# Random-feature attention: key and query products by halves of their stationary columns, values copied into rows of 65

## The chip, the cores and the metric

The kernel runs on one core of one Trainium2 chip. The metric is the device time of one execution in microseconds (us). Five engines with instruction streams of their own work together: TensorE (PE in the rows; its weight loads are PEld), VectorE (DVE), ScalarE (ACT), GpSimd (POOL) and SyncE (SP), whose queue issues the transfers. Each engine takes its own instructions in program order and waits on semaphores.

## The reference

Three parts follow each other: attention with positive random features, then a layer with `h - tanh(h)`, then four experts whose outputs are added with weights. Only the attention is touched:

```python
q_s, k_s = (q * scale, k * scale)
def phi(x):
    proj = np.einsum('bhsd,md->bhsm', x, omega)
    sq = np.sum(x * x, axis=-1, keepdims=True) / 2.0
    h = proj - sq
    h = h - np.max(h, axis=-1, keepdims=True)
    return np.exp(h) / np.sqrt(m)
q_p, k_p = (phi(q_s), phi(k_s))
kv = np.einsum('bhsm,bhsd->bhmd', k_p, v)
z = np.sum(k_p, axis=2)
num = np.einsum('bhsm,bhmd->bhsd', q_p, kv)
den = np.einsum('bhsm,bhm->bhs', q_p, z)[..., None] + 1e-06
return (num / den).astype(np.float32)
```

There are 2 batches, 8 heads, 576 rows, a head size of 64 and 128 features; everything is float32.

## The kernel before

Heads go in four pairs (p = 0 to 3). A batch's 576 rows are four tiles of 128 tokens and a rest of 64; the two batches' rests share one tile, so there are nine token tiles. The key stage runs first, pair by pair. `features` transposes the keys (tile `psT`), splits them into a high and a low part (`th` on ACT, `tl` on DVE), projects them (`psP`), takes the maximum (`nm` on DVE) and the exponent (`kf` on ACT). `k_products` then multiplies the features with the values: for each batch and head five float32 matmuls accumulate into `psV`, with 128 feature columns of `kf` stationary and 128 moving columns, 64 of them values and 64 of them ones, so that the sum z comes out beside kv. A DVE copy takes 96 of those 128 columns into `kvz[p]`.

The values lie in two tiles, `vs_105` for even pairs and `vs_106` for odd ones. Four transfers for a pair, a large one (line 199) and a small one for the rest rows (line 237) per batch, write straight into them, and the ones stand at the end of the same tile; `v_ones` makes the moving operand as a pattern of two blocks of 64. Pair p + 2 may be loaded once the matmuls of pair p have read the tile.

The query stage works on twelve units (a head pair and a third of the tiles). `turned` transposes query features (`psQ`, copied to `qt` on ACT); `attended` multiplies `qt` with `kvz` into `psN`: 128 stationary token columns and 96 moving columns for a tile of one batch (line 348). For the tile that holds both batches' rests it makes two matmuls of 64 stationary columns and 65 moving ones (line 352), one into the upper and one into the lower half of the partitions. DVE divides (`rd`, `xs`), and `back` turns the result over (`psX`).

Beside the key stage the first weights of the next layer are loaded into `raw` and decoded (ACT line 111, DVE lines 122, 126 and 127, split on ACT and POOL), and beside the query stage the first hidden products of that layer (`pse`, line 437) already run on PE. In these stages the order on each engine is decided by a scheduler from the program's dependences; in the layers behind them it is written by hand on PE, DVE and ACT.

Of the kernel before, what the change touches and what calls it, by code (L numbers as in the profile page):

```python
# [8 lines left out]
F32 = mybir.dt.float32  # L9
# [17 lines left out]
def tile_favor_attention__then__two_moe(  # L27
# [18 lines left out]
    nc = tc.nc  # L46
    B, H, S, D = q.shape
# [4 lines left out]
    P = 128  # L52
    NP = H // 2
    NT = N // P
    TB = S // P
# [14 lines left out]
    def split(hi, lo, src, eng_lo=None):  # L70
        nc.scalar.activation(hi, src, AF.Copy)
        (eng_lo or nc.vector).tensor_tensor(out=lo, in0=src, in1=hi.bitcast(F32), op=ALU.subtract)  # L72
# [110 lines left out]
    ac = actx.enter_context(tc.tile_pool(name="ac", bufs=1))  # L183
# [6 lines left out]
    kp = kctx.enter_context(tc.tile_pool(name="kp", bufs=2, side="right"))  # L190
    TD = TB * D
    VC = D + 1
    ZC = D + D // 2
    FULL = slice(0, TB * P)
    REST = slice(TB * P, S)

    def load_full(x, b, p, to):

        nc.sync.dma_start(out=to, in_=x[b, 2 * p:2 * p + 2, FULL, :].rearrange("h (r t) d -> r h (t d)", t=TB))
# [21 lines left out]
    kr = rests(k, "kr", kp)  # L221


    VR, VO = B * 2 * TD, B * 2 * (TD + D)
    vs = [kp.tile([P, VO + 3 * D], F32, tag=f"vs{i}", name=f"vs{i}", bufs=1) for i in range(2)]
    for i in range(2):
        nc.gpsimd.memset(vs[i][:, VR:], 0.0)
        nc.gpsimd.memset(vs[i][:, VO:VO + D], 1.0)
        for b in range(B):
            nc.gpsimd.memset(vs[i][b * D:(b + 1) * D, VO + (1 + b) * D:VO + (2 + b) * D], 1.0)  # L230

    def load_v(p):
        t = vs[p % 2]
        for b in range(B):
            load_full(v, b, p, t[:, b * 2 * TD:(b + 1) * 2 * TD].rearrange("p (h x) -> p h x", h=2))
            r = t[b * D:(b + 1) * D, VR + b * 2 * D:VR + (b + 1) * 2 * D].rearrange("p (h d) -> p h d", h=2)
            nc.sync.dma_start(out=r, in_=v[b, 2 * p:2 * p + 2, REST, :].rearrange("h r d -> r h d"))

    def v_ones(p, b, h, i):

        v0 = (b * 2 + h) * TD + i * D if i < TB else VR + (b * 2 + h) * D
        one = VO if i < TB else VO + (1 + b) * D
        x = vs[p % 2][:, v0:v0 + D]
        return bass.AP(x.tensor, x.offset, [x.ap[0], (one - v0, 2), x.ap[1]])

    load_v(0)
    kn.append(load_k(1))
    load_v(1)

    pso = ps_t.tile([P, 512], F32, tag="t", name="pso")  # L250
# [6 lines left out]
    for j in range(2):  # L257
        r, c = slice(j * D, (j + 1) * D), slice(j * P, (j + 1) * P)
        split(ob[0][r, c], ob[1][r, c], oms[r, :])
    qn = ac.tile([P, B, H, TD], F32, name="qn")  # L260
    kvz = [ac.tile([P, B, 2, ZC], F32, name=f"kvz{p}") for p in range(NP)]


    groups = [(0, 2), (2, 2), (TB, 1), (TB + 1, 2), (TB + 3, 2)]
# [43 lines left out]
    def k_products(p, kf):  # L308

        ps = ps_n.tile([P, B, 2, P], F32, tag="n", name="psV")  # L310

        def product(b, h):
            for i in range(TB + 1):
                nc.tensor.matmul(
                    ps[:, b, h, :], kf[:, TB if i == TB else b * (TB + 1) + i, h, :], v_ones(p, b, h, i),
                    start=i == 0, stop=i == TB,
                )
            if (b, h) == (B - 1, 1):
                nc.vector.tensor_copy(kvz[p], ps[:, :, :, :ZC])
                if p + 2 < NP:  # L320
                    load_v(p + 2)

        return [lambda b=b, h=h: product(b, h) for b in range(B) for h in range(2)]

    def q_products(p, gs, qf):

        nt = sum(n for _, n in gs)
        base = gs[0][0]
        xs = a3.tile([P, TB, 2, D], F32, tag="xs", name="xs")
        qt = {}  # L330

        def turned(g):
            t0, c = gs[g]
            ps = ps_t.tile([P, 2, 2, P], F32, tag="t", name="psQ")
            for j in range(c):
                for h in range(2):
                    nc.tensor.transpose(ps[:, j, h, :], qf[:, t0 - base + j, h, :], ident)
            qt[g] = a3.tile([P, 2, 2, P], F32, tag="qt", name="qt", bufs=4)
            nc.scalar.activation(qt[g][:, :c], ps[:, :c], AF.Copy)

        def attended(g):
            t0, c = gs[g]
            ps = ps_n.tile([P, 2, 2, P], F32, tag="n", name="psN")
            for j in range(c):
                t = t0 + j
                for h in range(2):
                    if t != TB:
                        nc.tensor.matmul(ps[:, j, h, :ZC], qt[g][:, j, h, :], kvz[p][:, t // (TB + 1), h, :], start=True, stop=True)  # L348
                        continue
                    for b in range(B):  # L350
                        r = slice(b * D, (b + 1) * D)
                        nc.tensor.matmul(ps[r, j, h, :VC], qt[g][:, j, h, r], kvz[p][:, b, h, :VC], start=True, stop=True)
            rd = a3.tile([P, 2, 2, 1], F32, tag="rd", name="rd")
            nc.vector.tensor_scalar(out=rd[:, :c], in0=ps[:, :c, :, D:VC], scalar1=1e-6 * M, scalar2=None, op0=ALU.add)
            nc.vector.reciprocal(rd[:, :c], rd[:, :c])
            nc.vector.tensor_tensor(
                out=xs[:, t0 - base:t0 - base + c], in0=ps[:, :c, :, :D], in1=rd[:, :c].to_broadcast([P, c, 2, D]), op=ALU.mult
            )

        def back():  # L360
            ps = ps_t.tile([P, 512], F32, tag="t", name="psX")
            for i in range(nt):
                nc.tensor.transpose(ps[:, i * P:(i + 1) * P], xs[:, i].rearrange("p h d -> p (h d)"), ident)
            c = slice(base * P, (base + nt) * P)
            split(xT[p][0][:, c], xT[p][1][:, c], ps[:, :nt * P])

        return (
            [lambda g=g: turned(g) for g in range(len(gs))], [lambda g=g: attended(g) for g in range(len(gs))], [back],
        )

# [4 lines left out]
    for p in range(NP):  # L375
        kf = kp.tile([P, NT, 2, M], F32, tag="xf", name="kf")
# [82 lines left out]
    def activated(i, j, eng_lo=None):  # L459
        new_g(i, j)  # L460
        hh, hl = gs[i, j]
        ps = ph[i, j][:, :, :CH]
        if i < NA:
            t, u, y = (late["gp"].tile([P, N], F32, tag=z, name=z, bufs=1 + (z == "y")) for z in "tuy")
            return minus_tanh(ps, hh, hl, t, u, y, grid, eng_lo)
        return [
            lambda: nc.scalar.activation(grid(hh), ps, AF.Relu),
            lambda: nc.vector.scalar_tensor_tensor(  # L468
                out=grid(hl), in0=ps, scalar=0.0, in1=grid(hh).bitcast(F32), op0=ALU.max, op1=ALU.subtract
            ),  # L470
        ]
# [234 lines left out]
    with tc.manual_schedule(engines={mybir.EngineType.DVE, mybir.EngineType.PE, mybir.EngineType.Activation}):  # L706
        coming = loads(0)
        opened(coming)
        g, left = None, []
        for n, (sh, so) in enumerate(order):  # L710
# [24 lines left out]
            g = activated(*steps[sh])  # L735
# [178 lines left out]
```

## Time and profile before

| what | us |
|---|---|
| median of three runs | 686.04 (684.09 to 686.70) |
| the profiled execution, its time | 686.23 |
| its span in the trace | 684.4 |
| PE busy | 668.2 |
| DVE busy | 528.5 |
| ACT busy | 317.2 |
| POOL busy | 61.3 |

The span runs from the first to the last recorded instruction; the execution's own time is 1.8 us longer. Busy times of PE come from modelled ends of matmuls that overlap, so a busy PE is not one at its peak. The attention takes the first 115 us or so, and the two layers the rest.

### The profile page before, as it was taken

The page shows a single profiled execution, that of the slowest core. Times are in us where ns is not written, and L with a number is a line of the kernel's source. Part 1 is how long each engine was busy: PE and PEld are TensorE (multiplying, and loading weights), DVE is VectorE, ACT ScalarE, POOL GpSimd, SP SyncE. Part 2 cuts the span into 40 slices and gives each one's busy share as a digit, 9 for nine tenths or more (in the row PEclk, how much of TensorE's full clock was granted, in tenths as well). Part 3 has the DMA queues.
Part 4 walks back from the last instruction along what each step waited for, and adds up shares of the span by engine and source line. Part 5 has one row for each costly group of instructions (what it writes and reads, how often), then busy time and mean ns, then how long its engine had stood idle before and what let it go on. Part 6 is the DMA issues. An engine that isn't in the chain of part 4 may idle for free.

```text
span 684.4 us, 10149 instructions
## 1 busy us (share of the span) xinstructions
PE 668.2 (98%) x4059; PEld 622.5 (91%) x4059; DVE 528.5 (77%) x824; ACT 317.2 (46%) x591; POOL 61.3 (9%) x58
## 2 busy tenths in 40 slices
PE   6999999999999999899999999999999999999997
PEld 5899989999999999799898899999988999999996
DVE  3599989799999977769477777777776878777664
ACT  4699988857757655435022222322232222232120
POOL 1032113413212200000000000000000000000000
PEclk9999999999999999999999999999999999999999
DMA  8853211012212222011001102120201110110004
GB/s 224 259 171 113 87 32 32 32 61 94 93 62 92 78 78 63 31 32 49 13 32 62 33 31 62 32 62 32 63 31 59 35 62 32 32 61 1 1 0 139
DMA packets 42767, 43.73 MB, mean 64 GB/s; under 512 B 5600, under 2 KB 37600, under 8 KB 42720
## 3 DMA queue, kind: packets, MB, share of 16 engines
q1 hardware_dynamic: 42720, 43.08, 20.2%
q8 instruction: 32, 0.52, 0.3%
q14 instruction: 15, 0.12, 0.1%
HBM read 40.72 MB, written 2.36 MB: 63 GB/s over the span
## 4 chain that ended last, share of the span: by engine, by line
PE 77%; DVE 13%; ACT 5%; issue 2%; DMA 2%; SPq 1%; DVEq 0%
PE po L665 29%; PE Y L648 23%; PE psh L437 7%; PE po L544 6%; PE pse L437 4%; PE psP L296 3%; PE psN L348 2%; DVE y L454 2%; DVE y L451 1%; DVE y L452 1%; DVE psh L453 1%; ACT y L448 1%; DVE m L127 1%; DVE m L126 1%; ACT m L117 1%
## 5 line engine op out<-in xcount | busy, mean ns | idle before, releaser
L671 DVE SCALAR_TENSOR_TENSOR oacc<-po,pr,oacc 128x512 f32<-128x512 f32 (+1 forms) x136 | 101.3, 746 | 34.2 <-PE po L665 33.8
L665 PE MATMUL po<-wbh,hl 128*128 128x512 f32 x290 | 113.0, 389 | 0.4 <-DVE hl L468 0.4
L665 PE MATMUL po<-wbh,hh 128*128 128x512 f32 x290 | 112.9, 389 | 0.1
L665 PE MATMUL po<-wbl,hh 128*128 128x512 f32 x290 | 112.9, 389 | 0.0
L665 PEld LDWEIGHTS po<-wbh,hl 128*128 128x128 f32 x290 | 54.4, 188 | 12.2 <-DVE hl L468 0.8
L665 PEld LDWEIGHTS po<-wbh,hh 128*128 128x128 f32 x290 | 54.7, 189 | 8.2 <-DVE oacc L671 0.3
L665 PEld LDWEIGHTS po<-wbl,hh 128*128 128x128 f32 x290 | 54.4, 188 | 7.5
L544 PE MATMUL po<-hh,wbh 128*128 128x384 f32 x180 | 60.8, 338 | 0.3
L826 ACT ACTIVATE hh<-Y 128x576 fp32r<-128x576 f32 x42 | 27.4, 653 | 72.5 <-DVE Y L823 64.0
L544 PE MATMUL po<-hh,wbl 128*128 128x384 f32 x180 | 60.5, 336 | 0.5 <-POOL wbl L72 0.5
L544 PE MATMUL po<-hl,wbh 128*128 128x384 f32 x180 | 60.7, 337 | 0.3 <-DVE hl L456 0.2
L648 PE MATMUL Y<-y,wah 128*128 128x288 f32 x336 | 57.9, 294 | 0.0
L437 PE MATMUL psh<-x,wah 128*128 128x384 f32 x288 | 57.7, 336 | 0.0
L648 PEld LDWEIGHTS Y<-y,wah 128*128 128x128 f32 x336 | 51.2, 188 | 3.6 <-DVE hl L468 0.3
L437 PEld LDWEIGHTS psh<-x,wah 128*128 128x128 f32 x288 | 50.5, 188 | 0.0
L648 PE MATMUL Y<-Th,wal 128*128 128x288 f32 x224 | 47.8, 295 | 0.0
L648 PE MATMUL Y<-Tl,wah 128*128 128x288 f32 x224 | 47.6, 294 | 0.0
L648 PE MATMUL Y<-Th,wah 128*128 128x288 f32 x224 | 47.6, 293 | 0.0
L826 ACT ACTIVATE hh<-u 128x576 fp32r<-128x576 f32 x14 | 9.6, 687 | 73.5 <-DVE u L823 73.5
L648 PEld LDWEIGHTS Y<-Th,wah 128*128 128x128 f32 x224 | 39.0, 188 | 4.5
L455 ACT ACTIVATE hh<-y 128x1152 fp32r<-128x1152 f32 (+3 forms) x24 | 20.3, 846 | 45.2 <-DVE y L454 45.2
L618 ACT ACTIVATE wah<-y 128x512 fp32r<-128x512 f32 x28 | 17.6, 631 | 41.1 <-DVE y L598 41.1
(138 smaller groups left out, 1472.5 us busy)
## 6 DMA issues: line engine op xcount, KB each, us to landing
raw<-in_moe_w_dram SPq DMA_DIRECT2D x30, 512.0 KB, 3.5
raw<-in_moe_w_in_dram SPq DMA_DIRECT2D x16, 512.0 KB, 3.6
raw<-in_moe_w_out_dram SPq DMA_DIRECT2D x16, 512.0 KB, 3.4
kn<-in_k_dram SPq DMA_DIRECT2D x8, 256.0 KB, 4.1
vs<-in_v_dram SPq DMA_DIRECT2D x8, 256.0 KB, 4.6
qn<-in_q_dram SPq DMA_DIRECT2D x8, 256.0 KB, 4.9
out_dram<-oacc SPq DMA_DIRECT2D x7, 256.0 KB, 2.3
raw<-in_moe_w_dram SPq DMA_DIRECT2D x4, 256.0 KB, 3.5
```

Of the source, the lines that this page charges most:

```text
L117: nc.scalar.activation(m, self.low.bitcast(U32), AF.Copy, scale=2.0**-29 * (1 - 2.0**-18), bias=-0.49999)
L296: nc.tensor.matmul(ps[:, i].rearrange("p a m -> p (a m)"), x[:, c], o, start=j == 0, stop=j == 2)
L348: nc.tensor.matmul(ps[:, j, h, :ZC], qt[g][:, j, h, :], kvz[p][:, t // (TB + 1), h, :], start=True, stop=True)
L437: nc.tensor.matmul(ph[i, j][:, n, :CH] if bank is None else bank, w[:, c], x[:, n * CH:(n + 1) * CH] if bank is None else x[:, n], start=z ...
L454: c=lambda: vec.copy_predicated(view(y), view(u).bitcast(I32), ps),
L455: h=lambda: act.activation(hh, y, AF.Copy),
L544: nc.tensor.matmul(po[:, :CH], w[:, r], g[:, s], start=j == 0 and z == 0, stop=j == NJ - 1 and z == 2,)
L618: nc.scalar.activation(w[0], src, AF.Copy)
L648: nc.tensor.matmul(ps[:, m, :HN // 2], w[:, kk], b[:, m * HN // 2:(m + 1) * HN // 2], start=first and kk == 0 and z == 0, stop=kk == 1 and ...
L665: nc.tensor.matmul(po, g[:, s], w[:, cols], start=j == 0 and z == 0, stop=j == 1 and z == 2)
L671: nc.vector.scalar_tensor_tensor(out=acc, in0=po, scalar=pr[:, t, e:e + 1], in1=acc, op0=ALU.mult, op1=ALU.add)
L826: nc.scalar.activation(halves(gs[NA + q, f][0][:, h * HN:(h + 1) * HN]), x, AF.Relu)
```

## The change

Every product of key features with values and of query features with `kvz` is made as two matmuls with 64 stationary columns each: one writes partitions 0 to 63 of the result, the other 64 to 127. Both have 65 moving columns, 64 of values (or kv) and one of ones (or z). To give the values a moving operand of 65 columns in a row, the two `vs` tiles now hold rows of 65 with a one behind each 64 values. The large transfers land in a new tile `vn` (three buffers), and GpSimd copies from it into `vs`; the small transfers of the rests still write into `vs`. `kvz` holds 65 columns, so the DVE copy into it takes 260 elements a partition in place of 384.

```diff
-    ZC = D + D // 2
+    HALVES = slice(0, D), slice(D, P)
...
     def load_v(p):
-        t = vs[p % 2]
+        x = vs[p % 2]
         for b in range(B):
-            load_full(v, b, p, t[:, b * 2 * TD:(b + 1) * 2 * TD].rearrange("p (h x) -> p h x", h=2))
-            r = t[b * D:(b + 1) * D, VR + b * 2 * D:VR + (b + 1) * 2 * D].rearrange("p (h d) -> p h d", h=2)
+            raw = kp.tile([P, 2, TD], F32, tag="vn", name="vn", bufs=3)
+            load_full(v, b, p, raw)
+            nc.gpsimd.tensor_copy(
+                x[:, b * 2 * TB:(b + 1) * 2 * TB, :D], raw.rearrange("p h (t d) -> p (h t) d", d=D),
+            )
+            r = x[b * D:(b + 1) * D, VS + 2 * b:VS + 2 * (b + 1), :D]
             nc.sync.dma_start(out=r, in_=v[b, 2 * p:2 * p + 2, REST, :].rearrange("h r d -> r h d"))
...
     def v_ones(p, b, h, i):
 
-        v0 = (b * 2 + h) * TD + i * D if i < TB else VR + (b * 2 + h) * D
-        one = VO if i < TB else VO + (1 + b) * D
-        x = vs[p % 2][:, v0:v0 + D]
-        return bass.AP(x.tensor, x.offset, [x.ap[0], (one - v0, 2), x.ap[1]])
+        return vs[p % 2][:, (b * 2 + h) * TB + i if i < TB else VS + 2 * b + h, :]
...
             for i in range(TB + 1):
-                nc.tensor.matmul(
-                    ps[:, b, h, :], kf[:, TB if i == TB else b * (TB + 1) + i, h, :], v_ones(p, b, h, i),
-                    start=i == 0, stop=i == TB,
-                )
+                for r in HALVES:
+                    nc.tensor.matmul(
+                        ps[r, b, h, :VC], kf[:, TB if i == TB else b * (TB + 1) + i, h, r], v_ones(p, b, h, i),
+                        start=i == 0, stop=i == TB,
+                    )
             if (b, h) == (B - 1, 1):
-                nc.vector.tensor_copy(kvz[p], ps[:, :, :, :ZC])
+                nc.vector.tensor_copy(kvz[p], ps[:, :, :, :VC])
...
                 for h in range(2):
-                    if t != TB:
-                        nc.tensor.matmul(ps[:, j, h, :ZC], qt[g][:, j, h, :], kvz[p][:, t // (TB + 1), h, :], start=True, stop=True)
-                        continue
-                    for b in range(B):
-                        r = slice(b * D, (b + 1) * D)
-                        nc.tensor.matmul(ps[r, j, h, :VC], qt[g][:, j, h, r], kvz[p][:, b, h, :VC], start=True, stop=True)
+                    for i, r in enumerate(HALVES):
+                        b = i if t == TB else t // (TB + 1)
+                        nc.tensor.matmul(ps[r, j, h, :VC], qt[g][:, j, h, r], kvz[p][:, b, h, :], start=True, stop=True)
```

The scheduler orders the attention anew. On PE, where the products of the first head pair (`psV` from `vs_105`) begin between the transposes and projections of the second, this stood before:

```order
L314 MATMUL psV<-vs_105,kf 128x128
L284 MATMUL psT<-ident,kn 128x128
L314 MATMUL psV<-vs_105,kf 128x128
L296 MATMUL psP<-ob_130,th 128x256
L296 MATMUL psP<-ob_131,th 128x256
L296 MATMUL psP<-ob_130,tl 128x256
L314 MATMUL psV<-vs_105,kf 128x128 x2
L296 MATMUL psP<-ob_130,th 128x256
```

and this stands there now:

```order
L316 MATMUL psV<-vs_105,kf 64x65 x2
L285 MATMUL psT<-ident,kn 128x128
L316 MATMUL psV<-vs_105,kf 64x65 x2
L297 MATMUL psP<-ob_138,th 128x256
L297 MATMUL psP<-ob_139,th 128x256
L297 MATMUL psP<-ob_138,tl 128x256
L316 MATMUL psV<-vs_105,kf 64x65 x4
L297 MATMUL psP<-ob_138,th 128x256
```

Nothing moved here except that one matmul became two: the products still stand in short runs between full-width matmuls. Over the whole program there are 31 such runs of `psV` halves (160 matmuls; run lengths from 2 to 14, and 10 of them odd).

In the query stage on PE, at the products of two successive head pairs with their `kvz` (behind the transposes `psQ` of query features), the order before was:

```order
L337 MATMUL psQ<-ident,qf 128x128 x4
L348 MATMUL psN<-kvz_140,qt 128x96 x4
L296 MATMUL psP<-ob_130,th 128x256
L296 MATMUL psP<-ob_131,th 128x256
L348 MATMUL psN<-kvz_141,qt 128x96
L363 MATMUL psX<-ident,xs 128x128 x4
```

and it is now:

```order
L339 MATMUL psQ<-ident,qf 128x128 x4
L351 MATMUL psN<-kvz_147,qt 64x65 x8
L351 MATMUL psN<-kvz_148,qt 64x65 x5
L297 MATMUL psP<-ob_138,th 128x256
L297 MATMUL psP<-ob_139,th 128x256
L351 MATMUL psN<-kvz_148,qt 64x65 x3
```

Here two products now stand in one run and one is cut after its fifth half; in all there are 27 runs of `psN` halves (144 matmuls; 10 runs are odd), where before there were five runs of line 352 with 16 halves.

On DVE, just ahead of the first decoding of weights (line 122), the maxima (`nm`) and the copies into `kvz` of the key stage stood so before:

```order
L298 TENSOR_REDUCE nm<-psP 128x4 x2
L72 TENSOR_TENSOR tl<-psT,th 128x128
L122 TENSOR_SCALAR m<-raw 128x512
L298 TENSOR_REDUCE nm<-psP 128x2
L126 SCALAR_TENSOR_TENSOR m<-y,m 128x512
L319 COPY kvz_140<-psV 128x384
L127 SCALAR_TENSOR_TENSOR m<-raw,m 128x512
L298 TENSOR_REDUCE nm<-psP 128x4 x2
```

and so now:

```order
L72 TENSOR_TENSOR tl<-psT,th 128x128
L299 TENSOR_REDUCE nm<-psP 128x4 x2
L321 COPY kvz_148<-psV 128x260
L299 TENSOR_REDUCE nm<-psP 128x2
L299 TENSOR_REDUCE nm<-psP 128x4
L122 TENSOR_SCALAR m<-raw 128x512
L299 TENSOR_REDUCE nm<-psP 128x4
L126 SCALAR_TENSOR_TENSOR m<-y,m 128x512
```

The second pair's copy into `kvz`, a maximum of two columns and one of four moved ahead of the first decoding.

On SP the queue ahead of the first `raw` transfer changed too: the large loads of the third pair's values no longer stand behind the end of the first pair's products but go out early; the two rest loads still stand there, and behind the second of them there are now six query loads instead of four before `raw`.

## Rows read from the trace of the kernel before

**Rows 1.** The page: span, busy time of two engines, the chain's shares by engine.
```profile
span 684.4 us, 10149 instructions
PE 668.2 (98%) x4059; PEld 622.5 (91%) x4059; DVE 528.5 (77%) x824; ACT 317.2 (46%) x591; POOL 61.3 (9%) x58
...
PE 77%; DVE 13%; ACT 5%; issue 2%; DMA 2%; SPq 1%; DVEq 0%
```

**Rows 2.** Busy time by stretch: length, PE, PEld, DVE, ACT, POOL, clock, DMA.
```profile
13.20:23.10 9.90, 9.90 (x84) 9.80 (x84) 5.56 (x10) 7.47 (x26) 0.00 (x0) 1.00 0.84 224
23.10:32.40 9.30, 8.68 (x74) 8.23 (x72) 4.16 (x8) 5.28 (x19) 0.00 (x0) 1.00 0.92 292
32.40:52.60 20.20, 18.77 (x156) 18.00 (x156) 20.17 (x35) 19.15 (x55) 6.44 (x5) 1.00 0.58 181
52.60:115.00 62.40, 62.34 (x477) 58.09 (x478) 56.59 (x148) 57.29 (x150) 13.08 (x11) 1.00 0.22 68
```

**Rows 3.** The chain that ended last, in order of time: start, us, what.
```profile
16.82 0.89 PE psV L314 x8
...
22.31 0.81 PE psP L296 x6
23.12 0.52 SPq L237
...
25.86 6.51 DMA raw<-in_moe_w_in_dram
...
69.09 0.87 PE psN L348 x8
...
74.31 0.38 PE psN L352 x8
74.69 0.66 PE pse L437 x2
...
78.11 0.38 PE psN L352 x8
78.49 0.66 PE pse L437 x2
...
87.55 1.84 PE pse L437 x8
```

**Rows 4.** Timeline of weight loads on PE around one run of line 352.
```profile
73.83 0.25 PEld L337 LDWEIGHTS psQ<-ident,qf 128*128 128x128 f32 x2
74.24 0.31 PEld L352 LDWEIGHTS psN<-kvz,qt 128*64 128x64 f32 x8 [0.16 <-issue]
74.62 0.19 PEld L437 LDWEIGHTS pse<-x,wah 128*128 128x128 f32 x1
```

**Rows 5.** Instructions of the tiles psV and psN: ns min/median/max, first and last start.
```profile
L314 PE MATMUL psV<-vs,kf x160: 270/275/421, 13.2 to 50.5; 128*128 128x128 f32 x160
L319 DVE COPY kvz<-psV x4: 542/546/557, 22.0 to 51.3; 128x384 f32<-128x384 f32 x4
...
L348 PE MATMUL psN<-kvz,qt x128: 243/275/351, 53.9 to 110.0; 128*128 128x96 f32 x128
L352 PEld LDWEIGHTS psN<-kvz,qt x32: 132/136/138, 74.2 to 91.4; 128*64 128x64 f32 x32
L352 PE MATMUL psN<-kvz,qt x32: 222/222/271, 74.2 to 91.5; 128*64 128x65 f32 x32
```

**Rows 6.** Groups on DVE from 20 to 36 us: busy, mean ns, idle before.
```profile
L298 DVE TENSOR_REDUCE nm<-psP 128x4 f32<-128x512 f32 x7 | 4.6, 687 | 1.6 <-PE psP L296 1.6
L122 DVE TENSOR_SCALAR m<-raw 128x512 int32<-128x512 int32 x2 | 1.7, 844 | 2.8 <-DMA raw<-in_moe_w_in_dram 2.8
...
L298 DVE TENSOR_REDUCE nm<-psP 128x2 f32<-128x256 f32 x2 | 0.8, 421 | 0.5 <-PE psP L296 0.5
```

**Rows 7.** SP's queue: start, us, issue.
```profile
3.71 0.62 SPq L199 DMA_DIRECT2D vs<-in_v_dram  x1
...
5.03 0.60 SPq L199 DMA_DIRECT2D vs<-in_v_dram  x1
...
21.79 0.37 SPq L199 DMA_DIRECT2D vs<-in_v_dram  x1
22.26 1.38 SPq L237 DMA_DIRECT2D vs<-in_v_dram  x1
23.69 2.12 SPq L199 DMA_DIRECT2D qn<-in_q_dram  x4
25.86 0.47 SPq L103 DMA_DIRECT2D raw<-in_moe_w_in_dram  x1
```

**Rows 8.** Issues between 3.6 and 4.4 us: size, median us to landing.
```profile
vs<-in_v_dram SPq DMA_DIRECT2D x1, 256.0 KB, 4.9
```

**Rows 9.** Groups on POOL up to 115 us: busy, mean ns, idle before.
```profile
L72 POOL TENSOR_TENSOR wal<-m,wah 128x512 fp32r<-128x512 f32 x5 | 7.1, 1418 | 49.7 <-ACT wah L71 49.7
...
L227 POOL MEMSET vs<- 128x448 f32 x2 | 1.0, 476 | 0.1
```

**Rows 10.** All instructions of line 122: ns min/median/max.
```profile
L122 DVE TENSOR_SCALAR m<-raw x11: 395/427/1512, 32.4 to 82.4; 128x512 int32<-128x512 int32 x11
```

More of the change, by code (lines that the diff above doesn't have):

```diff
@@ L221, in tile_favor_attention__then__two_moe @@
     kr = rests(k, "kr", kp)
[L224 to L228, printed above, removed]
+    VS = B * 2 * TB
+    vs = [kp.tile([P, VS + B * 2, VC], F32, tag=f"vs{i}", name=f"vs{i}", bufs=1) for i in range(2)]
+    for x in vs:
+        nc.gpsimd.memset(x[:, :VS, D:], 1.0)
+        nc.gpsimd.memset(x[:, VS:, :], 0.0)
         for b in range(B):
-            nc.gpsimd.memset(vs[i][b * D:(b + 1) * D, VO + (1 + b) * D:VO + (2 + b) * D], 1.0)
+            nc.gpsimd.memset(x[b * D:(b + 1) * D, VS + 2 * b:VS + 2 * (b + 1), D:], 1.0)
     def load_v(p):
-        t = vs[p % 2]
+        x = vs[p % 2]
         for b in range(B):
-            load_full(v, b, p, t[:, b * 2 * TD:(b + 1) * 2 * TD].rearrange("p (h x) -> p h x", h=2))
-            r = t[b * D:(b + 1) * D, VR + b * 2 * D:VR + (b + 1) * 2 * D].rearrange("p (h d) -> p h d", h=2)
+            raw = kp.tile([P, 2, TD], F32, tag="vn", name="vn", bufs=3)
[4 more added lines that the diff above has]
+            r = x[b * D:(b + 1) * D, VS + 2 * b:VS + 2 * (b + 1), :D]
             nc.sync.dma_start(out=r, in_=v[b, 2 * p:2 * p + 2, REST, :].rearrange("h r d -> r h d"))
     def v_ones(p, b, h, i):
-        v0 = (b * 2 + h) * TD + i * D if i < TB else VR + (b * 2 + h) * D
-        one = VO if i < TB else VO + (1 + b) * D
-        x = vs[p % 2][:, v0:v0 + D]
-        return bass.AP(x.tensor, x.offset, [x.ap[0], (one - v0, 2), x.ap[1]])
+        return vs[p % 2][:, (b * 2 + h) * TB + i if i < TB else VS + 2 * b + h, :]
     load_v(0)
@@ L260, in tile_favor_attention__then__two_moe @@
     qn = ac.tile([P, B, H, TD], F32, name="qn")
-    kvz = [ac.tile([P, B, 2, ZC], F32, name=f"kvz{p}") for p in range(NP)]
+    kvz = [ac.tile([P, B, 2, VC], F32, name=f"kvz{p}") for p in range(NP)]
     groups = [(0, 2), (2, 2), (TB, 1), (TB + 1, 2), (TB + 3, 2)]
```

## The prediction

> **What bounds the kernel now.** I read the page first [rows 1]: PE is busy for 98% of the span and stands for 77% of the chain that ended last, but such a share is an average, so the attention needs a view by stretch. The table of stretches [rows 2] cuts it where the chain changes hands, and each line shows another limit. From 13.2 to 23.1 us PE is busy for all of its 9.90 us. From 23.1 to 32.4 nothing is full; the chain of waits [rows 3] says why: the end of the first head pair's products releases a transfer in SP's queue at 23.12, behind it stand four query loads and then the first `raw` transfer, issued at 25.86 and landing 6.51 us later, and DVE idles 2.8 us for it [rows 6]. From 32.4 to 52.6 DVE is full (20.17 of 20.20 us) and PE nearly (18.77). From 52.6 to 115.0 PE is full again (62.34 of 62.40). Whatever the change does to PE thus counts in the first and last of these stretches, acts through SP's queue in the second, and can hide behind DVE in the third.
>
> **What a half costs.** The trace of before has halves already: line 352. A float32 matmul leaves two records (32 for 16 matmuls there, 160 for the 80 of `psV` [rows 5]). The timeline of weight loads [rows 4] shows eight records of line 352 in 0.31 us. One lasts 0.136 us [rows 5], so the last of the four steps starts some 0.17 us after the first, which is 0.058 us for a step of two records, one from either half. An upper and a lower half thus run side by side, and a pair takes two steps, 0.116 us. A whole matmul takes twice 0.111 us in `psV` (0.89 us for 8 records) and twice 0.109 us in `psN` (0.87 for 8) [rows 3]. A pair of halves saves about 0.1 us.
>
> **What the way in and out costs.** The same place shows the price. In the chain, eight records of line 352 and the two `pse` matmuls behind them take 0.38 + 0.66 = 1.04 us, twice alike [rows 3]. Two `pse` take 0.46 (1.84 us for 8), so the run of halves takes 0.58, of which four steps are 0.23. The other 0.35 us is paid once a run: PE's weight loads idle 0.16 us before the first half, for no reason but "issue", and the next full-width load comes only 0.38 us after the first half's [rows 4], without the overlap that loads have elsewhere. In line 352 as it stands, 0.58 us replaces two whole matmuls of 0.44. [...]
>
> **The sum on PE.** A run of n halves costs 0.35 + 0.116 for each pair begun.
> - `psV` before: 160 records x 0.111 = 17.8 us. Now 31 runs and, odd ones rounded up, 85 pairs: 10.85 + 9.86 = 20.7. That is +2.9 us.
> - `psN` before: 128 x 0.109 = 13.95, and line 352 with 5 runs and 9 pairs 1.75 + 1.04 = 2.8; together 16.75. Now 27 runs and 77 pairs: 9.45 + 8.93 = 18.4. That is +1.6 us.
>
> Pure streaming falls from 32.8 to 18.8 us, by 14.0, and 53 more runs eat that up where a run's price is over 14.0 / 53 = 0.264 us. I measured 0.35, so PE gets 4.5 us more work.
>
> **How much of it reaches the end, key stage.** The first head pair's products are cut into ten runs and a half (a run is shared with the second pair) with 21.5 pairs: 3.7 + 2.5 = 6.2 us against 40 x 0.111 = 4.4, so the release of SP's queue at 23.12 comes 1.7 us later. Behind it stand two more query loads (2.12 us for four [rows 7], so +1.06) and one large value load less (21.79 to 22.26, -0.47): `raw` lands about 2.3 us later. DVE, which is full from there, has less left to do then: the moved maxima and copy take 0.42 + 0.69 + 0.55 us [rows 5, 6], 1.66 together, and two later copies of 260 in place of 384 elements save some 0.13 each (a 256-wide operation takes 0.42 against 0.55). By DVE the stage ends 2.3 - 1.9 = 0.4 us later. By PE it ends 2.9 us later less the 2.05 us that PE idles between 23.1 and 52.6 [rows 2], so 0.85. The two wait on each other; I take 1.2. The bounds are 0.4, and 2.9 where no idle time can be used.
>
> **Query stage.** PE has no idle time there, so all of +1.6 counts. DVE and ACT are busy for 56.59 and 57.29 of 62.40 us and gain nothing to speak of.
>
> **The copies on GpSimd.** No row shows one. Eight copies of 512 elements lie between a memset of 448 (0.476 us) and a two-input operation on 512 (1.418) [rows 9]; with a strided target I take 1.2, nearer the latter. The first pair's large loads are issued at 3.71 and 5.03 [rows 7] and one lands after 4.9 us [rows 8], so at 8.6 and 9.9; at 1.42 each the copies end by 11.4, and the first `psV` starts at 13.2 [rows 5]. POOL has little else to do then (it idles for 49.7 us before its five splits of weights [rows 9]). This costs nothing; without that cover, each late microsecond would be one on PE, which is full. The fourth large load has to wait for the first copy (three buffers), and the keys of the third pair stand behind it; they then land near 16 us, ahead of the second batch's products, which start no sooner than 17.7 [rows 3]. The last pair's copies fall into DVE's full stretch. Line 122 takes 0.427 us in the median and up to 1.512 [rows 10], and if a copy on POOL were what stretches it, two would cost 2.2 us. I take 0 and keep 2.2 for the range.
>
> **Sum.** 1.2 + 1.6 = +2.8 us on 686.23, the profiled execution's own time (span 684.4), gives 689.0. The median of the runs, 686.04, is 0.2 lower; I stay at 689.0. That is 0.4%, below the 0.5% (3.4 us) that a measurement of this kernel can tell from no change.
>
> **Rivals.**
> - All 4.5 us are felt, because SP's queue and DVE leave PE no room, and the collisions on DVE add up to 2.2: 690.7 to 693. For it speaks that PE and DVE are both nearly full from 32.4 on; against it the 2.05 us of idle PE time. 0.20.
> - Hidden: the key stage takes up its share in that idle time, and the switches of the query stage fall where PE would have waited for `qt` anyway: 0 to +1, 686 to 687. Against it stands the query stage's 62.34 of 62.40. 0.14.
> - Faster, on the other side: a run's price is not the array's but that of line 352's place, say a wait for its operand. At 0.15 us a run, the query stage gains 6.1 - 22 x 0.15 = 2.8, the first pair 0.4, and DVE's lighter load behind `raw` brings 1.3 more: 4.5 us, 681.5. It decides from 0.264 us a run downwards and is measurable below about 0.2. Against it: two places with different work around them show the same 0.35, and the price is paid on the way out too. 0.12.
> - Pairs don't hold in longer runs. Line 352 shows only four steps in a row, and the new runs have up to 14 halves. Without any pairing 304 halves take 35.3 us and 58 runs 20.3, together 55.6 against 34.5: 707. For it speaks only that no row shows a longer run. 0.06. [...]
> - The forecast, 687 to 691: 0.48.
>
> **How the numbers follow.** Above 689.4 lies somewhat under half of the forecast's case (0.20), with the first rival and the last 0.46 slower by over 0.5%. The rest of the forecast (0.28) and the hidden case make 0.42 within it, and the faster rival 0.12. The range from 685.5 to 693.0 leaves out the last two rivals, 0.18.
>
> **What would show it.** In the trace of after: `psV` and `psN` halves in steps of about 0.058 us within a run; 58 runs, each with an idle of weight loads before its first load; `psV` ending later for the first pair by 1.7 us, and `raw` landing near 34.7; DVE full behind it; the query stage longer by 1.6 us, with the two layers behind it unchanged. I am wrong if the price of a run is clearly below 0.26 us, if long runs lose their pairing, or if GpSimd's copies appear among what PE waits for.

## The result, and the profile after

| | before | after |
|---|---|---|
| median, us | 685.13 (683.75 to 686.70, 6 runs) | 692.00 (690.67 to 694.84, 6 runs) |
| ratio | | 1.0104, 95% interval 1.0082 to 1.0127 |
| profiled execution: time, span | 686.23, 684.4 | 694.84, 693.0 |

The change costs 6.9 us, 1.0%. The forecast was +2.8 us, 689.0, with a range up to 693.0. The profiled execution of after is the longest of its runs (spans of 688.8 to 691.0 in the others). It holds two stretches of PE at half clock (0.50 granted), of which more at the end; its mean granted clock is 0.994, that of the others 0.998.

Two lines of the page of after, which answer to [rows 1]: PE is busy for 4 us more, with 288 more records (a float32 matmul leaves two: 320 for the 160 of `psV`). Only 1.1 us of the 4 lie between the first `psV` and the last `psN` (94.7 us before, 95.8 now); 2.8 lie behind the first `po`, where the half clock is (`po` is the layer's output product).

```profile
span 693.0 us, 10741 instructions
...
PE 672.3 (97%) x4347; PEld 616.1 (89%) x4347; DVE 530.1 (76%) x824; ACT 317.9 (46%) x591; POOL 65.8 (9%) x66
```

The stretches of [rows 2] in after (length, PE, PEld, DVE, ACT, POOL, clock, DMA share, GB/s):

```profile
13.20:23.10 9.90, 9.90 (x121) 7.98 (x121) 5.86 (x11) 7.07 (x25) 1.87 (x4) 1.00 0.69 206
23.10:32.40 9.30, 9.30 (x122) 7.58 (x124) 4.58 (x9) 6.14 (x22) 0.00 (x0) 1.00 0.79 252
32.40:52.60 20.20, 18.90 (x232) 15.98 (x233) 16.44 (x28) 17.25 (x51) 5.18 (x5) 1.00 0.57 179
52.60:115.00 62.40, 61.01 (x592) 51.81 (x591) 55.99 (x141) 57.69 (x149) 14.48 (x11) 1.00 0.20 61
```

DVE, full in the third stretch before, is busy for 16.44 of 20.20 us now. And where PE had almost no idle time from 52.6 us to 115 it has 1.4 us.

The tiles of [rows 5], and lines 237 and 122, in after (ns min/median/max, first and last start in us):

```profile
L316 PE MATMUL psV<-vs,kf x320: 219/222/272, 12.6 to 50.0; 128*64 128x65 f32 x160
L321 DVE COPY kvz<-psV x4: 412/418/429, 22.9 to 50.3; 128x260 f32<-128x260 f32 x4
...
L351 PE MATMUL psN<-kvz,qt x288: 219/222/272, 53.1 to 111.0; 128*64 128x65 f32 x144
...
L237 POOL COPY vs<-vn x8: 608/610/736, 8.4 to 37.4; 128x512 f32<-128x512 f32 x8
...
L122 DVE TENSOR_SCALAR m<-raw x11: 392/418/1489, 35.7 to 103.6; 128x512 int32<-128x512 int32 x11
```

The last key product starts at 50.0 us (50.5 before), the last query product at 111.0 (110.0). Up to there the change costs 1 us. The rest shows in the waits of PE behind it. These are all that PE waits for in after from 112 to 135 us; for the kernel before, the same view of 108 to 125 us has not one line.

```profile
PE po L543 <- DVE y L453: 2.0, 1, 2.0
PE pse L436 <- DVE y L453: 1.7, 1, 1.7
PE pse L436 <- DVE x L72: 0.9, 1, 0.9
```

Between the last `psN` and the first `po` both kernels give PE the same work: 72 records of `pse`, 4 of the transposes `psX` and 18 of `psh`. That takes 13.9 us before and 19.0 after, and 4.6 of the 5.1 us are these three waits. I call this stretch the hand-over. The same cuts for all kernels with the scheduler's order on PE, in us of the profiled executions (key: first `psV` to first `psN`; query: first to last `psN`; rest: first `po` to the end). Apart from the halves PE has the same records in each cut, but for two or four of `pse` in key halves and in the last kernel:

| kernel | key | query | hand-over | rest |
|---|---|---|---|---|
| before | 40.7 | 56.1 | 13.9 | 560.6 |
| after | 40.5 | 58.0 | 19.0 | 562.9 |
| after, profiled again | 39.4 | 57.3 | 19.0 | 562.3 |
| rows only, full width | 37.4 | 57.2 | 18.7 | 561.5 |
| key halves | 38.8 | 57.8 | 18.8 | 561.5 |
| query halves | 40.6 | 58.9 | 18.3 | 560.6 |
| before, hl first | 40.2 | 56.1 | 13.9 | 561.6 |
| after, hl first | 39.1 | 58.0 | 16.7 | 561.4 |
| rows only, hl first | 36.8 | 57.2 | 16.3 | 561.6 |
| query halves, hl first | 40.5 | 58.9 | 15.7 | 561.9 |
| after, three y | 38.8 | 58.0 | 18.8 | 561.4 |
| rows only, one decode later | 36.6 | 57.6 | 15.7 | 561.6 |

### The profile page after: what moved, and what is told of

The parts are those of the page before. It is cut to its first block, busy times and chain, and to the rows that moved or that the text cites. A ratio compares the mean times of both kernels' runs of the same rounds, so it can differ in the third digit from the quotient of the medians.

```text
span 693.0 us, 10741 instructions
## 1 busy us (share of the span) xinstructions
PE 672.3 (97%) x4347; PEld 616.1 (89%) x4347; DVE 530.1 (76%) x824; ACT 317.9 (46%) x591; POOL 65.8 (9%) x66
## 4 chain that ended last, share of the span: by engine, by line
PE 64%; DVE 10%; ACT 5%; issue 2%; DVEq 0%
PE po L664 28%; PE Y L647 22%; PE psh L436 7%; PE po L543 6%; DVE y L453 2%; DVE y L450 1%; DVE y L451 1%; DVE psh L452 1%; ACT y L447 1%; ACT m L117 1%; ACT u L446 1%; DVE m L127 1%; ACT y L111 1%; DVE m L126 1%; ACT wah L71 1%
## 5 line engine op out<-in xcount | busy, mean ns | idle before, releaser
L543 PEld LDWEIGHTS po<-hh,wbh 128*128 128x128 f32 x180 | 34.2, 190 | 3.1 <-DVE y L453 2.2
```

The source lines that it names most:

```text
L543: nc.tensor.matmul(po[:, :CH], w[:, r], g[:, s], start=j == 0 and z == 0, stop=j == NJ - 1 and z == 2,)
```

## The experiments

The first four were to separate the parts of the change, with a theory of late weights (D in the expectations: the first `raw` comes later, its decoding is pushed into the query stage and is missing at the end) against the plain one (P: PE has more to do).

**After, once more.** No edit.

> The changed kernel once more, unchanged, for a trace without the two clock drops of the first one (at 131 and 292 us). If the loss is made before 130 us, as theory D (the decoding of weights starts late, DVE lags, and PE waits for it where the query stage hands over to the next layer) and theory P (PE's 4.5 us of extra work) both say, the span is near 690 us and the clock stays at full speed. D says that PE waits for DVE line 453 for 4 to 6 us between 118 and 131 us again; P says that these waits are small, under 1.5 us.

692.69 us in one run. Its hand-over again has 4.4 us of waits, so they belong to the kernel and not to one execution.

**Rows only.** The copies, `vn` and rows of 65 stay; the products have 128 stationary columns again:

```diff
-                for r in HALVES:
-                    nc.tensor.matmul(
-                        ps[r, b, h, :VC], kf[:, TB if i == TB else b * (TB + 1) + i, h, r], v_ones(p, b, h, i),
+                nc.tensor.matmul(
+                    ps[:, b, h, :VC], kf[:, TB if i == TB else b * (TB + 1) + i, h, :], v_ones(p, b, h, i),
...
+                    if t != TB:
+                        nc.tensor.matmul(ps[:, j, h, :VC], qt[g][:, j, h, :], kvz[p][:, t // (TB + 1), h, :], start=True, stop=True)
+                        continue
```

> The changed kernel's rows of 65, GpSimd copies and order of transfers, with full-width products (128 stationary, 65 moving columns); halves stand only where they stood before. PE has no extra work. Theory D: the first weights still land late (seven query loads stand between the second rest load and them), by 1 to 2 us, and the kernel loses 1 to 3 us by waits at the hand-over near 120 us. Theory P: nothing is lost, 0 to -1 us.

688.37 us, ratio 1.0049 (1.0031 to 1.0066). The query products end 3.0 us earlier than before, and yet it is 3.3 us slower: the waits of its hand-over,

```profile
PE po L545 <- DVE y L455: 2.0, 1, 2.0
PE pse L438 <- DVE y L455: 1.4, 1, 1.4
PE pse L438 <- DVE x L72: 1.0, 1, 1.0
```

are nearly those of after. A kernel without one new half pays them, so extra work on PE isn't their cause.

**Key halves.** As rows only, with the halves in `psV` alone.

> As the changed kernel, but the query products at full width with 65 moving columns: only the key products are halves (31 runs, 85 pairs). PE has 2.9 us more work than before, all in the key stage. Theory D: +4 to +6 us, nearly all of the change's loss less the query stage's 1.6, with PE waiting for DVE line 453 near 120 us. Theory P: +1 to +3 us, the key stage ending later by that and no such waits.

690.47 us, 1.0080 (1.0057 to 1.0103): 2.1 us over rows only, of which 1.4 lie in the key stage; the two intervals overlap.

**Query halves.** The values, `kvz` and key products of before; only `attended` makes halves:

```diff
-                    if t != TB:
-                        nc.tensor.matmul(ps[:, j, h, :ZC], qt[g][:, j, h, :], kvz[p][:, t // (TB + 1), h, :], start=True, stop=True)
-                        continue
-                    for b in range(B):
-                        r = slice(b * D, (b + 1) * D)
+                    for i in range(2):
+                        r = slice(i * D, (i + 1) * D)
+                        b = i if t == TB else t // (TB + 1)
```

> The kernel before with its values and key products as they were, and only the query products by halves (30 runs, 81 pairs): PE has 30 x 0.35 + 81 x 0.116 = 19.9 us against 16.75, +3.1 us, in the query stage alone, and the first weights land as before (32.4 us). Theory P: +3.1 us. Theory D: +2 to +3 us from the same cause, with no new wait at the hand-over, since the decoding is on time.

692.23 us, 1.0098 (1.0076 to 1.0120): 7.2 us lost, where both theories expected 2 to 3.1. Its query stage grew by 2.8. Its first weights are decoded on time (line 122 from 31.5 to 84.0 us, before 32.4 to 82.4 [rows 10]) and the hand-over has 3.7 us of waits for DVE all the same. The theory of late weights falls.

What the four have in common is that the scheduler set the order of every engine anew. On GpSimd three splits `wal` of weights of the layer's next unit stand among the last `hl` (the low part of `y` in `early`), and DVE decodes one or two of those weights among the same groups. The hand-over on GpSimd in after (start, us, instruction, idle before):

```profile
120.52 1.45 POOL L72 TENSOR_TENSOR wal<-m,wah 128x512 fp32r<-128x512 f32 x1 [3.06 <-ACT wah L71]
121.93 1.48 POOL L455 TENSOR_TENSOR hl<-y,hh 128x384 fp32r<-128x384 f32 x1
124.60 1.61 POOL L72 TENSOR_TENSOR wal<-m,wah 128x512 fp32r<-128x512 f32 x1 [1.20 <-issue]
126.17 1.01 POOL L455 TENSOR_TENSOR hl<-y,hh 128x384 fp32r<-128x384 f32 x1
128.38 1.27 POOL L72 TENSOR_TENSOR wal<-m,wah 128x512 fp32r<-128x512 f32 x1 [1.20 <-issue]
```

In the kernel before these splits stand among the `hl` as well, but one `hl` later, so that two of them and not three start ahead of the first `po` at 123.9 us; and DVE's last decoding (line 127 at 108.4 us) is over when the hand-over begins:

```profile
117.35 1.03 POOL L456 TENSOR_TENSOR hl<-y,hh 128x384 fp32r<-128x384 f32 x1 [1.84 <-ACT hh L455]
118.66 1.30 POOL L72 TENSOR_TENSOR wal<-m,wah 128x512 fp32r<-128x512 f32 x1 [0.28 <-ACT wah L71]
120.46 1.02 POOL L456 TENSOR_TENSOR hl<-y,hh 128x384 fp32r<-128x384 f32 x1 [0.50 <-ACT hh L455]
122.68 1.29 POOL L72 TENSOR_TENSOR wal<-m,wah 128x512 fp32r<-128x512 f32 x1 [1.20 <-issue]
```

In after, ACT waits there for `hl`, since `y` has two buffers, three times and 3.3 us in all:

```profile
ACT y L447 <- POOL hl L455: 3.3, 3, 1.6
```

So the next theory, O, was that this order costs about 3.5 us, whatever the halves do. Its rival, W: DVE's decoding there sets the pace, and GpSimd only waits along. The test sets the order on GpSimd alone:

```diff
-    for e in range(NU - NP, NU):
-        early(e)
-        if e < NU - 2:
+    with tc.manual_schedule(engines={mybir.EngineType.Pool}):
+        for e in range(NU - NP, NU):
+            early(e)
+        for e in range(NU - NP, NU - 2):
             ready(load_a, wa, 1, e % NJ + 1)
```

It moves these rows of after on GpSimd, and beyond them one `hh` against one `m` on ACT:

```
-L455 TENSOR_TENSOR hl<-y,hh 128x384 x2
-L72 TENSOR_TENSOR wal<-m,wah 128x512
-L455 TENSOR_TENSOR hl<-y,hh 128x384
-L72 TENSOR_TENSOR wal<-m,wah 128x512
-L455 TENSOR_TENSOR hl<-y,hh 128x384
-L72 TENSOR_TENSOR wal<-m,wah 128x512
+L455 TENSOR_TENSOR hl<-y,hh 128x384 x4
 L455 TENSOR_TENSOR hl<-y,hh 128x256 x4
+L72 TENSOR_TENSOR wal<-m,wah 128x512 x3
```

**After, hl first.**

> The changed kernel; on GpSimd alone the order of the last stretch of the attention is set: the three splits wal of the next unit's weights stand behind all hl, not among them. DVE and PE keep their order row by row, ACT but for one row. Theory O (in every re-ordered kernel wal stands ahead of hl on GpSimd, ACT waits there for the y buffer that hl holds, and PE for ACT's and DVE's chain: 3.8 to 4.9 us of PE gaps ahead of the first po in four kernels, none in the one before): the gaps of PE for DVE y ahead of the first po fall from 3.7 us to under 1, the first po comes some 3.5 us sooner relative to the last psN (from 19.0 to 15.5), and the time falls from 692.0 to 688 to 689. Rival W (PE itself got the work and DVE's decoding in the tail sets the pace, GpSimd only waits along): no change, 691 to 693.

688.91 us, 1.0056 (1.0043 to 1.0069), 3.1 us less than after; the intervals don't touch. So W alone is not the cause. In the profiles the hand-over is 2.4 us shorter (16.65 against 19.01), and the 2.7 us over the kernel before that stay are not touched by this test: there W remains possible. The row of ACT moves along in every kernel with hl first, so what it is worth is not separated. The waits for `y` fall from 3.7 to 1.4 us:

```profile
PE pse L436 <- DVE x L72: 0.9, 1, 0.9
PE po L544 <- DVE y L453: 0.8, 1, 0.8
PE pse L436 <- DVE y L453: 0.6, 1, 0.6
```

**Rows only, hl first.**

> The copies and the rows of 65 with products of full width (688.4 us), and GpSimd's hl ahead of wal in the tail. Theory O: its 3.4 us of PE gaps for DVE y go, 684.5 to 685.5, level with the kernel before or a little under it; the key stage was 4.2 us shorter there, of which 3 us show at the last psN. Rival W: 688 to 689.

684.79 us, 0.9997 (0.9987 to 1.0006): 3.6 us less than rows only, and level with before.

**Query halves, hl first.**

> The kernel before with halves in the query products alone (692.2 us), and GpSimd's hl ahead of wal in the tail. Theory O: the two gaps of 1.2 and 2.5 us that PE waits for DVE y go, 688 to 689; what is left over the kernel before is the 2 to 3 us that the query stage grew by. Rival W: 691.5 to 693.

690.50 us, 1.0075 (1.0060 to 1.0089). It gains 1.7 us where 3 to 4 were expected, and the intervals touch, so its time alone would not carry the theory. Its hand-over shortens by 2.6 us, as in the other two pairs (2.4 each); the rest is 1.3 us longer in its profile, which has 3.4 us of half clock at 286.6 us where that of query halves has none.

**Before, hl first.**

> The kernel before, with hl ahead of wal on GpSimd in the same place. It has no PE gap there, so theory O expects no change, 684.5 to 686. If it gets faster by over 1.5 us, the order has a value of its own that the trace of before doesn't show; if it gets slower, late wal costs something (the products of the next unit wait for it) and the other three runs carry that cost too.

685.20 us, 1.0002 (0.9993 to 1.0011): the order is worth nothing where PE didn't wait, and late splits cost nothing.

**After, three y.** The order stays as in after; only the buffer for which ACT waits is added:

```diff
-        t, u, y = (a2.tile([P, 512], F32, tag=z, name=z)[:, :w] for z in "tuy")
+        t, u, y = (a2.tile([P, 512], F32, tag=z, name=z, bufs=2 + (z == "y"))[:, :w] for z in "tuy")
```

> The changed kernel with three buffers in place of two for the y of the hidden products that run inside the attention. No engine's order changes by a row; GpSimd still has the three splits among its hl. Theory O in its full form (ACT waits for the y buffer that hl holds, because wal stands ahead of hl): ACT's two waits of 1.6 and 1.4 us for hl go and with them most of what the other order brought, 688.5 to 690. If the y pair is not the link (hl is waited for by something else), 691 to 693.

691.57 us, 1.0104 (1.0084 to 1.0123): nothing gained. ACT no longer waits for GpSimd at all, and PE's waits are 4.4 us, in after 4.6. So the link in theory O was wrong, though the order is the cause. What takes its place stands in two timelines of this kernel, GpSimd's and DVE's:

```profile
121.02 1.47 POOL L72 TENSOR_TENSOR wal<-m,wah 128x512 fp32r<-128x512 f32 x1
122.45 1.52 POOL L455 TENSOR_TENSOR hl<-y,hh 128x384 fp32r<-128x384 f32 x1
123.97 1.29 POOL L72 TENSOR_TENSOR wal<-m,wah 128x512 fp32r<-128x512 f32 x1
125.21 0.93 POOL L455 TENSOR_TENSOR hl<-y,hh 128x256 fp32r<-128x256 f32 x1
```

```profile
120.58 0.76 DVE L450 SCALAR_TENSOR_TENSOR y<-y,u 128x256 f32<-128x256 f32 x1
121.27 1.25 DVE L517 TENSOR_SCALAR sm<-sm 128x9 f32<-128x9 f32 x1
122.44 0.68 DVE L127 SCALAR_TENSOR_TENSOR m<-raw,m 128x512 int32<-128x512 int32 x1
...
124.23 1.30 DVE L450 SCALAR_TENSOR_TENSOR y<-y,u 128x256 f32<-128x256 f32 x1
125.46 0.73 DVE L519 TENSOR_TENSOR pr<-pr,sm 128x36 f32<-128x36 f32 x1
```

An operation on nine elements a partition (line 517) takes 1.25 us. It starts at 121.27, 0.25 us into a split on GpSimd, and ends at 122.52 as that split does (122.49). Line 519 starts 0.25 us into the `hl` at 125.21 and ends with it, 126.19 against 126.14. The other way round, the `hl` at 122.45 starts with line 127 and takes 1.52 us in place of 1.03. These are the same operations in the timeline of DVE in "after, hl first" (its lines from 505 on are numbered one higher), where GpSimd idles between its `hl`:

```profile
121.38 0.41 DVE L450 SCALAR_TENSOR_TENSOR y<-y,u 128x256 f32<-128x256 f32 x1
121.71 0.17 DVE L518 TENSOR_SCALAR sm<-sm 128x9 f32<-128x9 f32 x1
...
123.92 0.43 DVE L450 SCALAR_TENSOR_TENSOR y<-y,u 128x256 f32<-128x256 f32 x1 [0.24 <-ACT y L447]
124.27 0.19 DVE L520 TENSOR_TENSOR pr<-pr,sm 128x36 f32<-128x36 f32 x1
```

The excess is 0.35 + 1.08 + 0.87 + 0.54 = 2.8 us on DVE, about what ACT had waited. Not every operation of DVE lasts longer there: beside the `hl` at 122.45, lines 451 and 452, which read `pse` from PSUM, keep their 0.41 and 0.42 us and the reciprocal of line 518 its 0.20. What decides it, these rows do not show. With two buffers ACT waits for GpSimd, with three DVE's operations last longer beside it, and the end is the same. What the two have in common, and the kernels with hl first do not, is three splits of 1.3 to 1.6 us on GpSimd in that stretch, right beside DVE. That this is how the order costs its time is read from these rows; no run tested it.

**Sixteen runs, and its control.** Is it the number of runs that makes halves lose? In rows of 65 with hl first, PE's key stage is put in program order, where the five products of a batch and head stand together; one kernel makes them by halves, in 16 runs in place of 31, the other at full width:

```diff
-    post = []
+    post, held = [], ExitStack()
+    held.enter_context(tc.manual_schedule(engines={mybir.EngineType.PE}))
...
+    held.close()
     kctx.close()
```

> Copies, rows of 65, halves in the key products alone, hl ahead of wal in the tail; on PE the key stage runs in program order, so that the five products of a batch and head stand together: 16 runs of 10 halves in place of 31 runs. If the price of a run is what made the halves lose (0.35 us a run, 0.116 a pair), their PE time is 16 x 0.35 + 80 x 0.116 = 14.9 us against 160 x 0.107 = 17.1 for full width in the same order, and this kernel is level with or up to 2.2 us faster than the next one. If halves cost more by themselves, whatever their runs, it is 1 us or more slower than the next one. The absolute time, with an order that waits where the scheduler's did not, is open: 682 to 689.

> The control of the one before: the same order on PE, full-width products of 65 moving columns. Its distance to the kernel with scheduled order and hl ahead of wal (684.8) is what the program order costs or brings by itself: 682 to 688. Price theory: 0 to 2.2 us above the run before; the other: 1 us or more below it.

No row stands beside the 0.107 us that the first of the two reckons for a full-width record; in rows only the loads of such records are 0.11 us apart. Halves 692.46 us (690.03 to 694.82), full width 695.96 (692.30 to 697.65); ratios 1.0111 (1.0090 to 1.0132) and 1.0162 (1.0143 to 1.0182). The order itself costs 6 us or more (spans of 690.5 and 684.3 us for full width with and without it, medians further apart), since PE now waits for ACT in the key stage (6.3 and 5.2 us ahead of `psP`). In that order halves are not slower, so "halves cost by themselves" falls. How much faster they are stays open: both times scatter by 5 us, the full-width runs had the lower mean clock (0.987 to 0.999, the halves 0.992 to 1.0), and the profiled key stages are alike (43.5 us), that of the halves with a mean clock of 0.91 from 24 to 60 us.

**Rows only, one decode later.** Rows only, hl first, with three `y`, and the second weight of the hand-over decoded in the layer behind it:

```diff
+    held = (load_a(1, 2), wa, (1, 2))
+    held[0].scaled()
...
+        held[0].joined()
+        parted(*held)
```

> Copies and rows of 65 with products of full width, hl ahead of wal on GpSimd (684.8 us so far), and two things more: three buffers for y, and one of the two weights that DVE decoded in the last stretch of the attention is decoded behind it, in the layer. The kernel at 684.8 still had three PE gaps there, 2.06 us: 1.00 for DVE's x, late because line 126 stood ahead of it and took 1.5 us beside an hl, 0.28 and 0.78 for y. If the last stretch is set by what DVE and GpSimd do there together, the gaps fall under 1 us and the time to 683 to 684.3, faster than the kernel before by 0.1 to 0.3%. If the decoding moved into the layer is waited for there (the products of the next unit need that weight), it is 684.5 to 687.

685.23 us, 0.9991 (0.9981 to 1.0001), where 683 to 684.3 was expected if the theory held. PE's waits fall from 2.1 to 1.6 us, the time does not move. Nor did the decoding: the weight that was moved is still decoded ahead of the first `po` (lines 126 and 127 at 118.7 and 120.0 us), and lines 122, 126 and 127 take 3.4 us of the hand-over against 3.5 in rows only, hl first. So this run is no test of what DVE's decoding costs there. No version beats the kernel before by more than can be measured.

## Why the prediction was right in its range, and where its sum was wrong

692.0 lies in the stated range, but beyond the forecast's own case of 687 to 691, and what filled the range is not what it was widened for. That the range held is luck; what held of the mechanism is the price of a half.

**The price of a half and of a run: right.** This timeline row of after is a run of 18 records; the first starts at 16.45, the last 0.66 - 0.14 = 0.52 us later, after nine steps of 0.058 us.

```profile
16.45 0.66 PEld L316 LDWEIGHTS psV<-vs,kf 128*64 128x64 f32 x18
```

Of the 58 runs, 48 have a full-width matmul ahead of them and two behind; what they take beyond 0.058 us a step, up to the second of the two, is 0.35 us in the median. The rivals "faster" (0.15 us a run) and "pairs don't hold" fall by that. Against full width with the same 65 columns and the same order on GpSimd the halves cost 688.91 - 684.79 = 4.1 us.

**The sum on PE, +4.5: too large.** From the first `psV` to the last `psN` PE is busy for 94.7 us before, 93.5 in rows only and 95.8 in after. The halves add 2.3 us to full width of 65 columns, and 1.1 to the kernel before; that 65 columns at full width would take 1.1 us less than the kernel before was not in the sum.

**The query stage, +1.6: right in number, not in what it is made of.** In the four executions with these products it grew by 1.3 to 1.9 us. In after, PE is busy for only 0.5 us more and idles for 1.4, where the prediction saw no room for idle time and the kernel before has none; 1.2 of that are two waits, for `tl` (DVE) and `qf` (ACT). Rows only, without a new half, grew by 1.1.

**The copies on GpSimd at no cost: right,** and cheaper than thought, 0.61 us where 1.2 was the estimate. `psV` began at 12.6 us, before at 13.2.

**The key stage, +1.2: wrong in sign and size.** In four executions with these products it took 38.8 to 40.5 us, before 40.2 and 40.7. The term that was mis-sized is what rows only changes (copies, rows of 65 and the orders that came with them): the sum gave a few tenths for it, and it takes 40.7 - 37.4 = 3.3 us away, with hl first 40.2 - 36.8 = 3.4. Of the 3.3, 1.6 are idle time of PE (2.1 us before, 0.55 in rows only). To rows only the halves add 1.4 us (key halves), 2.0 and 3.1 (after, twice) or 2.3 (both with hl first), about as much as the 2.9 of the sum. Full-width loads behind each other don't show why 65 columns save PE time; in rows only, 14 loads are (1.64 - 0.20) / 13 = 0.11 us apart, as with 128 columns:

```profile
19.30 1.64 PEld L315 LDWEIGHTS psV<-vs,kf 128*128 128x128 f32 x14
```

What else shortens that stage was not taken apart. The chain through SP's queue gave the forecast number by another way: `raw` was decoded from 35.7 us, told 34.7, before 32.4. But the first pair's copy into `kvz` starts 0.9 us later (22.9 against 22.0) and not 1.7, and the second rest load 0.6 later; it is issued at 22.26 before [rows 7], not at the 23.12 that the prediction took from the chain. The first `raw` is issued 0.84 us later, and then lands after 9.0 us in place of 6.5:

```profile
22.85 0.61 SPq L241 DMA_DIRECT2D vs<-in_v_dram  x1
23.50 3.16 SPq L199 DMA_DIRECT2D qn<-in_q_dram  x6
26.70 0.47 SPq L103 DMA_DIRECT2D raw<-in_moe_w_in_dram  x1
```

"DVE full behind it" did not come: DVE had 3.8 us to spare from 32.4 to 52.6.

**"The two layers behind it unchanged": right for the layers, and the step that failed is the one it hides.** From the first `po` on, query halves takes 560.6 us as the kernel before does; every profile with 561.4 or more in that column has half clock in that stretch, before with hl first (561.6) too. But the sum had only a key and a query stage. It took the hand-over between them and the layers as given, at its 13.9 us, and it was the largest term: +5.1 us in both profiles of after, whose spans are 8.5 and 6.4 us longer. Of these, 2.4 us are shown to be the place of three `wal` on GpSimd: where they stand behind `hl`, they are gone, with or without halves (in the medians 3.1, 3.6 and 1.7). In the kernel before, where they stand one `hl` later and DVE has no decoding left, moving them changes nothing. So the order costs time only together with something else, and whether that is the decoding no run separates.

The other 2.7 us go with DVE's decoding: what stood ahead of 110 us before stands among the last groups now, and `x` comes 0.9 us late behind a line 126 that took 1.52 us beside an `hl` (the next one took 0.76). With the splits behind `hl`, the hand-over takes 13.9 us (before) and 14.0 (the control of the sixteen runs) where DVE decodes nothing in it, 15.0 with 0.7 us of decoding (sixteen runs), 15.7 with 1.4 (query halves), 15.7 and 16.3 with 3.4 and 3.5 (rows only, with and without the later decode) and 16.7 with 3.6 (after). These kernels differ in more than that, and no run took the decoding away by itself, so it is read from the traces and not shown.

**The account,** in medians. Rows, copies and hl first: -0.4 us. The halves: +4.1. The scheduler's order on GpSimd: +3.1. Together +6.8, measured +6.9; they are the steps from kernel to kernel, so that they add up by construction. The rival that came nearest, "all 4.5 us are felt and the collisions add up to 2.2", had the right range for another reason: the collisions between DVE and GpSimd are there (2.8 us of DVE's time in "after, three y"), at the other end of the attention.

## What to carry to other kernels

Where a scheduler sets the order, a change is also a new order for stretches that it doesn't touch: compare each engine's order up to the next hand-written stage, and cost the stretch in which one stage hands over to the next as a stage of its own. By the prices measured here, halves of 64 columns are worth the price of a run only where it has more than three pairs or so (0.35 us against 0.1 saved a pair); runs of five pairs were no slower than full width, but no gain clear of the scatter was measured. A buffer added for a wait brought nothing here, since the engine waited for had no time left (GpSimd works without a gap from 118.17 to 126.14 us in three `y`); look at how long its neighbours' operations take, not only at the waits. And when a run is meant to move work, look in its trace whether the work has moved.

## What the runs showed of the hardware

The collision of DVE with GpSimd above shows as busy time and not as a wait: an operation on nine elements that takes 1.25 us ("after, three y", line 517) in place of 0.17 ("after, hl first", line 518) is how the trace tells of it.

In the profile of after PE's granted clock fell to half (0.50) for 3.4 us, twice, at 131.44 and at 291.86 us. The first stretch, with PE, PEld, DVE, ACT, POOL and the clock:

```profile
131.44:134.86 3.42, 3.42 (x13) 3.42 (x12) 2.69 (x7) 3.42 (x9) 1.31 (x2) 0.50 0.00 0
```

Ahead of it PE had idled 4.6 us in three waits. "After, profiled again" fell for 6.8 us at 126.07, behind two waits of 0.9 and 1.8 us; rows only, key halves and three `y`, with 4.4 to 4.9 us of waits at the same place, did not fall there. The second stretch does not come from the change: nine of the fourteen profiled executions, before with hl first among them, fall for 3.4 us between 282 and 292 us, behind two waits of PE of 1.2 and 0.95 us, and the other five have the same two waits and keep the full clock. Where no other stretch of half clock lies between the first and the last `po`, the rest takes 561.4 to 561.9 us with that stretch and 560.1 to 560.6 without, so it costs about 1 us. Two kernels whose profiles differ in it cannot be compared by their spans alone.
